# Softmax denominators by a transposing DMA and GpSimd in place of TensorE and VectorE, in an attention-then-MoE kernel on one Trainium2 core

## The chip, the cores and the metric

The kernel runs on one core of one Trainium2 chip. The metric is device time in microseconds, the median of the runs. Before the change it is 327.26 us, with runs from 327.18 to 327.89 us.

## The reference

For each of B = 4 batches there are N = 12544 rows of x with C = 128 channels, and m = 32 inducing vectors. An attention block is applied twice, and a small MoE layer follows.

```python
def mab(q, kv):
    s = scale * (q @ kv.transpose(0, 2, 1))
    s = s - s.max(-1, keepdims=True)
    a = np.exp(s)
    a /= a.sum(-1, keepdims=True) + 1e-09
    return a @ kv
h = mab(I, x)          # 32 rows per batch: I attends to x
y = mab(x, h)          # 12544 rows per batch: x attends to h
out = np.maximum(y @ w1, y @ w2) @ w_out      # d_ff = 1024
```

The denominators of the title are the sums over 32 entries in the second `mab`, one for each of the 50176 rows of x. They can be divided out at the very end, since all that follows is positively homogeneous.

## The kernel before

**Algebra.** max(h1, h2) is written as h1 + relu(h2 - h1). With H the 32 rows of h, the kernel makes `hwd` = H (w2 - w1), 32x1024, and `m1` = H w1 w_out, 32x128. For each chunk of 128 rows of x it needs E = exp(scores) (32x128), relu(hwd^T E) in eight pieces of 128 rows, the product of these with w_out, plus m1^T E, and at last a division by the denominators.

**Tiles.** A batch has 98 chunks. Up to 16 chunks make a block, four for each quarter of the 128 partitions: quarter q of tile `e2` (128x512, f16) has in its 32 partitions the exps of up to four chunks. There are 28 blocks, seven for each batch, numbered 0 to 27.

**Stages of a block.** `stage` (L577) multiplies the transposed x by H on TensorE (L591), and ScalarE makes `e2` by an exp (L603). `phase` (L932) issues four small products at a time, one in each quarter of TensorE's rows (L990). They give relu inputs in PSUM, which ScalarE (L1006) or VectorE (L1009) moves to SBUF, and also the product with `m1`. `final_one` (L797) issues the product with w_out, one matmul of 128 rows by 128 columns at a time (L809), up to 32 for a group of four chunks. `evict_group` (L826) multiplies the group by the reciprocal denominators `rp` on VectorE (L836) into an output tile `o`, and an output DMA on SyncE's queue (L861) sends it to HBM.

**The denominators.** `dens` (L626) is called by the first `final_one` of a block. For each chunk column it loads 128 columns of `e2` as weights and multiplies them by `ones_q` (128x4), so that four sums for 128 rows of x come out in PSUM (L641). It does two blocks at once where the next one is staged. VectorE takes the reciprocals (L651) into `rp`.

**The first attention** of batch b+1 runs beside the second attention of batch b. GpSimd's queue loads x by `load_x` (L160 to L165): seven DMAs per batch, which turn f32 into f16. They start after the copy L164, which waits for the last accumulation of the batch in hand (`pool_accum`, L348 to L403). SyncE's queue turns x by fourteen transposing DMAs per batch (L171), and the exps `eu` by six more (L345). Scores are made at L308, `pool_accum` at L364.

**What sets the order.** The program is recorded by hand. A planner keeps a clock of its own (`Clock`, L20), with a cost for each operation, and decides from it what TensorE does next: a phase, an output matmul, a block's staging or a piece of the first attention. A table `DEV` (L901) overrides single steps. Engines then take their instructions in the recorded order, and so do the queues: SyncE issues its DMAs one after the other, and a DMA that waits holds all that stand behind it. A tile pool with n buffers makes the first write of a buffer wait until the tile that had it n allocations ago is released. The output tiles have five buffers:

```python
outp = ctx.enter_context(tc.tile_pool(name="outp", bufs=5))
```

So the VectorE instruction that evicts a group waits until the output DMA of the group five before it has landed.

## Time and profile before

The profile is of one execution on the chip. The page gives its span, first to last instruction; its own time beyond the span isn't listed.

| what | before |
|---|---|
| median of three runs (lowest, highest) | 327.26 us (327.18, 327.89) |
| span of the profiled execution | 325.6 us |
| TensorE (PE) busy, share of the span | 319.8 us, 98% |
| VectorE (DVE) busy | 283.1 us, 87% |
| ScalarE (ACT) busy | 281.7 us, 87% |
| GpSimd (POOL) busy | 25.6 us, 8% |
| granted TensorE clock | 1.000 |
| DMA, mean over the span | 165 GB/s |

The page sums busy time by engine, follows back the chain of work that ended last, lists groups of instructions by line, and lists the DMA issues with the median time from issue to landing. PEld is TensorE's weight load, SPq SyncE's queue. A group's row reads: line, engine, operation, output and inputs with shapes, count, then busy time and mean ns of one, then idle time before it and what ended it. A row of the timeline begins with the start in us from the span's start and the duration in us.

### The profile page before, as it was taken

The numbers are of one execution on the slowest core, as the hardware profiler recorded it, in microseconds if no ns is written. First come the engines' busy times: TensorE is split into PE (matmuls) and PEld (weight loads), VectorE is DVE, ScalarE is ACT, GpSimd is POOL, SyncE is SP. The second block draws the span as 40 slices with busy tenths as digits, with TensorE's granted clock in tenths as the row PEclk, the third lists the DMA queues.
The fourth block names the chain that finished last, engine by engine and source line by source line (L and its number), as shares of the span: only waits on it lengthen the run. The fifth ranks groups of instructions, "written<-read, shape, count | busy, mean of one in ns | idle before, by whom it ended". The sixth has DMA issues, their size and how long they took to land.

```text
span 325.6 us, 12570 instructions
## 1 busy us (share of the span) xinstructions
PE 319.8 (98%) x5404; PEld 243.0 (75%) x5404; DVE 283.1 (87%) x509; ACT 281.7 (87%) x560; POOL 25.6 (8%) x51
## 2 busy tenths in 40 slices
PE   7999999999999999999999999999999999999996
PEld 3876777777767777777777777777777777778785
DVE  3359989989989998998989999998989999999973
ACT  3679899999989899998888999989969999999961
POOL 7452030000040000000040000000000000000000
PEclk9999999999999999999999999999999999999999
DMA  8999999976279999993389999992312312222233
GB/s 204 208 206 214 286 246 212 172 207 134 97 150 245 225 248 209 201 203 86 116 162 243 214 234 232 190 192 86 115 66 101 113 68 98 90 108 99 85 115 112
DMA packets 70823, 53.65 MB, mean 165 GB/s; under 512 B 52176, under 2 KB 55408, under 8 KB 70768
## 3 DMA queue, kind: packets, MB, share of 16 engines
q1 hardware_dynamic: 64656, 38.63, 49.2%
q0 software_dynamic: 6112, 14.22, 22.3%
q8 instruction: 42, 0.69, 0.9%
q14 instruction: 13, 0.11, 0.1%
HBM read 28.33 MB, written 25.69 MB: 166 GB/s over the span
## 4 chain that ended last, share of the span: by engine, by line
PE 95%; DVE 1%; DMA 1%; ACT 0%; issue 0%; ACTq 0%; DVEq 0%
PE ps L809 61%; PE ps L990 22%; PE ps L591 2%; PE ps L232 2%; PE ps L308 2%; PE ps L364 1%; DMA xf<-in_x_dram 1%; PE ps L248 1%; DVE relu L1009 1%; PE ps L280 1%; PE ps L641 1%; PE ps L766 1%; PE ps L271 1%; PE ps L657 0%; PE ps L473 0%; PE ps L409 0%
## 5 line engine op out<-in xcount | busy, mean ns | idle before, releaser
L1006 ACT ACTIVATE relu<-ps 128x512 f16<-128x512 f32 x461 | 244.8, 602 | 26.6 <-PE ps L990 18.1
L1009 DVE TENSOR_SCALAR relu<-ps 128x512 f16<-128x512 f32 x323 | 206.8, 682 | 16.9 <-PE ps L990 15.3
L809 PE MATMUL ps<-woutp,relu 128*128 128x128 f16 x3136 | 217.3, 220 | 0.0
L809 PEld LDWEIGHTS <-relu 128*128 128x128 f16 x3136 | 176.7, 98 | 39.6 <-issue 29.1
L990 PE MATMUL ps<-e,hwd 32*128 32x512 f16 (+2 forms) x880 | 88.7, 360 | 0.0
L836 DVE TENSOR_TENSOR o<-ps,rp 128x512 f32<-128x512 f32 (+3 forms) x108 | 68.5, 634 | 5.5 <-PE ps L809 3.4
L990 PEld LDWEIGHTS <-hwd 32*128 32x128 f16 x880 | 24.9, 91 | 21.1 <-issue 1.0
L990 PE MATMUL ps<-m,e 32*128 32x128 f16 x381 | 38.8, 217 | 0.0
L990 PEld LDWEIGHTS <-e 32*128 32x128 f16 x381 | 21.3, 93 | 2.6
L165 POOL DMA_DIRECT2D xn<-in_x_dram x31 | 17.0, 557 | 8.2 <-DMA xn<-in_x_dram 4.3
L236 DVE COPY xT<-ps 128x512 f16<-128x512 f16 (+3 forms) x11 | 5.5, 504 | 7.8 <-PE ps L232 7.7
L319 ACT ACTIVATE eu<-ps 128x512 f16<-128x512 f32 x18 | 10.8, 615 | 0.0
L603 ACT ACTIVATE e<-ps 128x512 f16<-128x512 f32 (+2 forms) x21 | 10.5, 577 | 0.0
L164 POOL COPY pace<-hacc 128x1 f32<-128x1 f32 x2 | 0.4, 184 | 114.8 <-DVE hacc L397 114.8
L591 PE MATMUL ps<-xT,hT 128*32 128x512 f16 (+3 forms) x114 | 8.9, 362 | 0.0
L239 ACT COPY xT<-ps 128x768 f16<-128x768 f16 (+3 forms) x11 | 6.1, 556 | 2.7 <-PE ps L232 2.6
L232 PE MATMUL ps<-identity,xn 128*128 128x128 f16 x98 | 7.4, 219 | 0.4 <-DVE xn L661 0.3
L232 PEld LDWEIGHTS <-xn 128*128 128x128 f16 x98 | 5.6, 97 | 1.6 <-DVE xn L661 1.1
L257 ACT ACTIVATE et<-ps 128x448 f16<-128x448 f32 (+4 forms) x11 | 4.5, 413 | 2.6 <-PE ps L248 2.6
L308 PE MATMUL ps<-xT,inducingT 128*32 128x512 f16 x72 | 6.5, 385 | 0.0
L591 PEld LDWEIGHTS <-hT 128*32 128x32 f16 x114 | 3.3, 94 | 4.1 <-issue 3.0
L364 PE MATMUL ps<-xn,eT 128*32 128x128 f16 x288 | 5.5, 220 | 0.0
(96 smaller groups left out, 108.2 us busy)
## 6 DMA issues: line engine op xcount, KB each, us to landing
out_dram<-o SPq DMA_DIRECT2D x90, 256.0 KB, 2.4
xn<-in_x_dram POOLq DMA_DIRECT2D x24, 448.0 KB, 11.8
out_dram<-o SPq DMA_DIRECT2D x10, 128.0 KB, 3.0
xn<-in_moe_w_dram POOLq DMA_DIRECT2D x4, 256.0 KB, 14.1
xn<-in_x_dram POOLq DMA_DIRECT2D x4, 224.0 KB, 10.2
xT<-xn SPq DMA_TRANSPOSE x42, 4.3
xf<-in_x_dram SPq DMA_DIRECT2D x1, 512.0 KB, 3.9
xf<-in_x_dram SPq DMA_DIRECT2D x1, 384.0 KB, 4.3
```

Of the source, the lines that this page charges most:

```text
L165: nc.gpsimd.dma_start(out=xn_at[b, i][:, 0:n, :], in_=xr[b, :, k0 : k0 + n, :])
L232: nc.tensor.transpose(ps[:, j, :], xn[:, g + j, :], identity16)
L308: nc.tensor.matmul(out=ps[32 * g : 32 * (g + 1), :], lhsT=inducingT, rhs=xT_tiles[b % 2][:, U * u + 4 * g : U * u + 4 * (g + 1), :], start ...
L319: nc.scalar.activation(out=eu, in_=ps, func=AF.Exp, scale=scale, accum_out=st[b]["es"][:, u : u + 1])
L364: nc.tensor.matmul(out=ps[32 * g : 32 * (g + 1), 0:128], lhsT=eT[:, j, 32 * g : 32 * (g + 1)], rhs=xn_of(b, U * v + 4 * g + j), start=(j = ...
L591: nc.tensor.matmul(out=ps[32 * q : 32 * (q + 1), 128 * t : 128 * (t + n)], lhsT=hq, rhs=xT[:, c : c + n, :], start=True, stop=True, tile_p ...
L603: nc.scalar.activation(out=blk.e2[:, 0 : 128 * wd], in_=ps[:, 0 : 128 * wd], func=AF.Exp, scale=st[0]["rs"] if blk.b == 0 else scale,)
L809: nc.tensor.matmul(out=g.ps[:, 128 * c : 128 * (c + 1)], lhsT=g.blk.relu[q][:, 128 * (jb * w4 + t) : 128 * (jb * w4 + t + 1)], rhs=woutp[: ...
L836: nc.vector.tensor_mul(osb[:, 0:n, :], g.ps[:, 0 : n * C].rearrange("p (s c) -> p s c", s=n), rp)
L990: nc.tensor.matmul(**seq[i])
L1006: nc.scalar.activation(out=dst, in_=src, func=AF.Relu)
L1009: nc.vector.tensor_scalar(out=dst, in0=src, scalar1=0.0, scalar2=None, op0=ALU.max)
```

## The change

From block 3 on, `dens` is not called. When a block has been staged, `turn_e2` issues a transposing DMA on SyncE's queue that turns `e2` into `ed` (two buffers): 128 rows of x on the partitions, and for each chunk column the four quarters' 32 exps along the row. GpSimd adds halves of 16, 8, 4, 2 and 1 entries (five instructions, through the tile `half`, which has one buffer), and a sixth raises the sums to the power -1 into `rd` (seven buffers), which takes the place of `rp` in `evict_group`. A block's turn is switched on by `turns_on`, a job that is due when 18 chunks are done, and which now also issues the subtraction `weights_1b` that stood before the main loop. Some constants (identity32, rep32, diag, the inducing vectors) move into a buffer that the relu tiles use later, which makes room in SBUF; `ones16` shrinks to two columns and `ones32`, which nothing read, goes.

```diff
+    edp = ctx.enter_context(tc.tile_pool(name="edp", bufs=2))
...
-    identity32 = consts.tile([128, 128], F32, name="identity32")
-    ones32 = consts.tile([128, 128], F32, name="ones32")
-    ones16 = consts.tile([128, 128], F16, name="ones16")
+    head = relup.tile([128, 4096], F16, name="head", tag="relu3").bitcast(F32)
+    identity32 = head[:, 0:128]
+    rep32 = head[:, 128:256]
+    ind_sb = head[0:M, 256:384]
+    diag = head[:, 384:416]
+    ones16 = consts.tile([128, 2], F16, name="ones16")
...
+    minus1 = consts.tile([128, 16], F32, name="minus1")
...
+        state = {"turn": False}
+
         def stage(blk):
...
             blk.staged = ck.bank[bi] = ck.on_act(end, 0.05 + wd * 128 / 1200.0)
+            if state["turn"]:
+                turn_e2(blk)
             blk.staged = max([blk.staged] + [st[qu.b].get("hwdr", 0.0) for qu in some])
+
+        def turn_e2(blk):
+
+            wd = blk.width
+            uid[0] += 1
+            ed = edp.tile([128, 4, 128], F16, name=f"ed_{uid[0]}", tag="ed")
+            nc.sync.dma_start_transpose(
+                ed[:, 0:wd, :], blk.e2[:, 0 : 128 * wd].rearrange("p (j t) -> p j t", j=wd)
+            )
+            den = edp.tile([128, 16], F32, name=f"den_{uid[0]}", tag="den")
+            half = edp.tile([128, 16, 16], F32, name=f"half_{uid[0]}", tag="half", bufs=1)
+            cur = ed[:, 0:wd, :].rearrange("p j (q m) -> p (j q) m", q=4)
+            n = M // 2
+            while n >= 1:
+                dst = half[:, 0 : 4 * wd, 0:n] if n > 1 else den[:, 0 : 4 * wd, None]
+                nc.gpsimd.tensor_tensor(out=dst, in0=cur[:, :, 0:n], in1=cur[:, :, n : 2 * n], op=ALU.add)
+                cur = half[:, 0 : 4 * wd, :]
+                n //= 2
+            rp = edp.tile([128, 4, 4], F32, name=f"rd_{uid[0]}", tag="rd", bufs=7)
+            nc.gpsimd.tensor_tensor(
+                out=rp[:, 0:wd, :].rearrange("p t q -> p (t q)"),
+                in0=den[:, 0 : 4 * wd],
+                in1=minus1[:, 0 : 4 * wd],
+                op=ALU.pow,
+            )
+            blk.rp = rp[:, 0:wd, :]
+            blk.turned = blk.staged
...
+        def turns_on():
+            weights_1b()
+            state["turn"] = True
...
         pending = []
+        at(18, turns_on)
...
+            if f is turns_on:
+                return True
...
         state["stage"] = 2
-        weights_1b()
         START = ck.pe
```

More of the change, by code (lines that the diff above doesn't have):

```diff
@@ L176 @@
     identity16 = consts.tile([128, 128], F16, name="identity16")
-    identity32 = consts.tile([128, 128], F32, name="identity32")
-    ones32 = consts.tile([128, 128], F32, name="ones32")
-    ones16 = consts.tile([128, 128], F16, name="ones16")
+    head = relup.tile([128, 4096], F16, name="head", tag="relu3").bitcast(F32)
[4 more added lines that the diff above has]
+    ones16 = consts.tile([128, 2], F16, name="ones16")
     warm = consts.tile([128, 512], F16, name="warm")
     ones_q = consts.tile([128, 4], F16, name="ones_q")
-    ind_sb = consts.tile([M, C], F32, name="ind_sb")
+    minus1 = consts.tile([128, 16], F32, name="minus1")
     w2h = relup.tile([128, 4096], F16, name="w2h", tag="relu0")[:, 0:J]
@@ L191 @@
     m1bd = consts.tile([128, 4, C], F16, name="m1bd")
-    rep32 = consts.tile([128, 128], F32, name="rep32")
     repd = consts.tile([128, 128], F32, name="repd")
-    diag = consts.tile([128, M], F32, name="diag")
     pace = consts.tile([128, 1], F32, name="pace")
@@ L214 @@
         nc.vector.memset(ones16, 1.0)
-        nc.vector.memset(ones32, 1.0)
+        nc.vector.memset(minus1, -1.0)
         nc.vector.memset(ones_q, 0.0)
@@ L724 @@
             g.blk.last_group[g.q] = n
-        state = {"g": 0, "mm": 0, "lin": 0, "done": 0, "issued": 0}
+        state.update({"g": 0, "mm": 0, "lin": 0, "done": 0, "issued": 0})
         ptr = [[0, 0] for _ in range(4)]
@@ L1046 @@
         pending = []
+        at(18, turns_on)
         def ready(f, a):
-            d = st[a[0]]
+            d = st[a[0]] if a else None
             now = ck.pe
+            if f is turns_on:
+                return True
             if f is pool_scores and a[1] >= NEU and ("eT", a[1] - NEU) not in d:
```

## The prediction

> **What bounds the kernel now.** I read the busy shares and the chain on the page first, then the groups by shape, the timeline where a denominator is made, and the DMA lists of single windows, since the change puts work on queues.

> ```profile
> PE 319.8 (98%) x5404; PEld 243.0 (75%) x5404; DVE 283.1 (87%) x509; ACT 281.7 (87%) x560; POOL 25.6 (8%) x51
> PE 95%; DVE 1%; DMA 1%; ACT 0%; issue 0%; ACTq 0%; DVEq 0%
> ```

> TensorE is the bound over the whole span: 95% of the chain is its own work, and it waits for almost nothing. So TensorE time taken away comes off the end, and a stall put in is added in full. VectorE and ScalarE have an eighth of their time free.

> **What goes.** These are the groups by shape, and the timeline of TensorE around eight denominator matmuls.

> ```profile
> L641 PE MATMUL ps<-ones_q,e 128*128 128x4 f16 x102 | 4.7, 165 | 0.0
> L651 DVE RECIPROCAL rp<-ps 128x32 f32<-128x32 f32 x9 | 3.1, 348 | 0.0
> L522 POOL TENSOR_TENSOR w<-xn,xn 128x512 f16<-128x512 f32 x2 | 2.5, 1270 | 10.3 <-DMA xn<-in_moe_w_dram 10.3
> ```

> ```profile
> 59.90 0.34 PE L641 MATMUL ps<-ones_q,e 128*128 128x4 f16 x8
> ...
> 60.11 0.27 PE L809 MATMUL ps<-woutp,relu 128*128 128x128 f16 x2
> ```

> The 165 ns of one matmul overlap. Eight of them delay the next output matmul from 59.90 to 60.11, so one costs 0.21 / 8 = 26 ns. The built program keeps 12 of the 102 (blocks 0 to 2), so 90 x 26 ns = **2.3 us** go. VectorE loses 13 of 15 reciprocals, some 13 x 0.32 = 4.2 us, and a PSUM bank is taken 13 times less. As nothing on TensorE waits for these, I count zero; at most they give 0.5 us.

> **What moves.** With dens gone the planner's clock runs differently. In the built order TensorE goes to column mode (staging, first attention) in three more visits; the rest of its counts stands. A change of mode leaves weight loads idle some 0.23 us (29.1 us over 124 waits "PEld L809 <- issue" in the list of waits). An extra visit costs one more change, and fewer returns elsewhere pay part: 0.4 us, between 0 and 0.7.

> **What is added.** There are 25 turns: 25 transposing DMAs on SyncE's queue and 150 GpSimd instructions. GpSimd's price has no row of its shape. The copy of one column took 184 ns (L164), the 512-column L522 1270 ns, so a line through both gives 2.1 ns per column: 0.73, 0.45, 0.32, 0.25, 0.22 us for the five adds and 0.22 for the power, 2.2 us in all. Bounds are six copies, 1.1 us, and six L522, 7.6 us. Over 325 us GpSimd has room. Nor is `rd` late by itself: the exps of blocks 7 to 10 begin at 93.9, and block 7's first eviction is at 108.2, the shortest such distance of a turned block.

> The cost is in **SyncE's queue**. `ed` has two buffers. Where three or four blocks are staged in a row, the third DMA must wait until the first has landed and GpSimd has read it, and the fourth for the second. All output DMAs behind them wait too, and with five `o` buffers the fifth eviction after the first held output stops VectorE, relus behind it included. So it counts how fast a turn lands. The first rows below are of the whole run; then come two lines of the issues between 90 and 113 us, while x for batch 2 is loaded; then DMA packets between 178.5 and 180.5 us, when a transpose runs beside the loads of batch 3.

> ```profile
> out_dram<-o SPq DMA_DIRECT2D x90, 256.0 KB, 2.4
> ...
> xT<-xn SPq DMA_TRANSPOSE x42, 4.3
> ...
> eT<-eu SPq DMA_TRANSPOSE x18, 2.8
> ```

> ```profile
> xn<-in_x_dram POOLq DMA_DIRECT2D x7, 448.0 KB, 13.1
> out_dram<-o SPq DMA_DIRECT2D x4, 256.0 KB, 8.0
> ```

> ```profile
> DMA packets 212, 0.43 MB, mean 214 GB/s; under 512 B 14, under 2 KB 103, under 8 KB 212
> ...
> q0 software_dynamic: 107, 0.37, 92.8%
> q1 hardware_dynamic: 105, 0.06, 13.9%
> ```

> A turn of 128x512 f16 is like eT: 2.8 us in quiet. Beside the loads the two queues get one packet each in turn, 105 against 107 in 2 us, 53 per us, whatever their size. Transposes move in 256-byte packets: 42 xT of 224 KB and 18 eT of 128 KB make 46848, and the page has 52176 packets under 512 B. A turn has 512, and needs 512 / 53 = **9.7 us** beside the loads.

> [...] The counts above speak for one against one.

> **Window A, 94 to 117 us.** In both programs blocks 7 to 10 are staged after the 664th output matmul, just behind the seven loads of batch 2 (issued 90.4 to 94.1, the last landing 19.6 us later, at 113.2). First turn: issued at 94.5, behind two outputs of 128 packets each, which are through between 96.8 (256 packets at 53 per us from 92) and 101.3 (issue of the second plus 8.0). I take 99; it lands at 108.7. GpSimd's first add ends at 109.4. The second turn gets the last of the loads' time and lands at about 112.2, the next add ends at 112.9, the fourth turn's issue (1.2 us, as eT's) at 114.1, and the first held output, issued in 0.3 us, lands 2.4 us later at 116.8. Which eviction waits for it:

> ```profile
> 95.03 0.42 DVE L836 TENSOR_TENSOR o<-ps,rp 128x256 f32<-128x256 f32 x1 [0.15 <-PE ps L809]
> ...
> 105.77 0.42 DVE L836 TENSOR_TENSOR o<-ps,rp 128x256 f32<-128x256 f32 x1
> ```

> The eviction of 95.03 is the first whose output stands behind the turns, and that of 105.77 is the fifth after it. VectorE is held from 105.8 to 116.8, 11.0 us. TensorE goes on for one round of a phase and output matmuls (1.1 us in the chain, phases at 105.99 and 107.14); the next phase needs the bank of the held eviction. Loss **9.9 us**, between 3 (turns landing twice as fast) and 13.

> **Window B, 165 to 183 us.** The new order makes batch 2's last accumulation after the 1356th output matmul (1381st before), so the loads of batch 3 start at about 161.3 and end by about 181. Blocks 14 to 16 are staged after the 1389th (1422nd before), exp at 165.1 instead of 167.9. First turn: 165.1 + 9.7 = 174.8, add 0.7, third turn issued at 176.8. Its outputs stand behind the second and third turn in the DMA queue, and the first lands at about 182.7. The fifth eviction, at 175.75 before, is held 6.9 us. Loss **5.8 us**, between 1 and 9.

> **Elsewhere** three turns in a row stand at blocks 21 to 23 and 24 to 26, with no loads about: the third waits 2.8 + 0.7 us, which five buffers bear. Between 47 and 66 us SyncE is full (outputs are issued up to 6 us behind their evictions), and the two turns put ahead of batch 1's tenth xT transpose delay it by 2 x 1.2 us. It landed at 59.5, and scores at 60.9 use it. For this and the like in batches 2 and 3 I add 1.5 us, between 0 and 4.

> **The sum**: -2.3 + 0.4 + 9.9 + 5.8 + 1.5 = +15.3 us on the profiled execution. Its span of 325.6 us lies 1.7 below the median of 327.26, and I add the change to the median: **342.6 us**. With all lower ends it is 328.5 (-2.8 + 0 + 3 + 1 + 0), with all upper ones 351.7 (-2.3 + 0.7 + 13 + 9 + 4).

> **Rivals.** First, the other side: the turns land in time and the gain stays. This is decided at window A: VectorE isn't held if 94.5 + L + 0.7 (add) + 1.5 (rest of that block's chain) + 0.7 + 1.2 + 0.3 + 2.4 is under 105.8, so if a turn lands in L < 4.5 us. For it speaks eT's 2.8 us (4.2 at most); against it that no eT was issued beside loads, and outputs there took 8.0. It gives 327.26 - 2.3 + 0.4 = 325.4 us. Second, only one window bites, since in B the queue starts empty and the third turn may go sooner: 327.26 - 2.3 + 0.4 + 9.9 + 1 = about 336. Third, GpSimd is slow: the power or the strided adds have no row. At the bound of 7.6 us per block the fourth turn goes out 5 us later and A costs 15: about 348. That the change doesn't do what it says is excluded by the built order: 12 denominator matmuls, 25 turns.

> **Chances.** Forecast 0.68 (333 to 351), one window 0.14 (328.5 to 337), slow GpSimd 0.05, hidden 0.13, in which small delays may eat the gain. From these: faster 0.10, same 0.03, slower 0.87, where 0.2% is about what a measurement of this kernel can tell from no change. The range 328.5 to 350 takes in the first two.

> **What would show it.** After: an eviction near 106 us that waits about 10 us for an output DMA, TensorE idle in that slice and near 176; a turn's landing median near 3 us but 10 us beside loads; output matmuls after L641 gone. Turns landing under 4.5 us beside loads would make it wrong.

## The result, and the profile after

The changed kernel takes 352.83 us (median of 5 runs, 352.26 to 353.45); the kernel before took 327.30 us beside it. The ratio is 1.077, with a 95% interval from 1.075 to 1.079. The change makes the kernel 25.5 us slower. The profiled execution took 352.83 us, with a span of 351.1 us.

The page, with the rows that answer to those shown of before, and with TensorE and its granted clock over the span in 40 slices of 8.8 us (a digit is tenths of busy time, or of full clock; 9 is 90% or more):

```profile
PE 323.8 (92%) x5314; PEld 243.9 (69%) x5314; DVE 281.2 (80%) x496; ACT 281.4 (80%) x560; POOL 137.1 (39%) x201
PE   8999999999992299999999199999999999999996
PEclk9999999999998589999999589999999999999999
PE 77%; DMA 13%; DVE 4%; POOL 2%; ACT 1%; issue 1%; SPq 1%; DVEq 0%; ACTq 0%
```

TensorE runs 90 matmuls less, yet is busy 4.0 us longer. Two holes stand out, in slices 13 and 14 and in slice 23, and in or just behind each the granted clock is lowered. In the chain, TensorE's share falls from 95% to 77% and DMA's rises from 1% to 13%. The list of waits names who waits in the holes (total, times, longest):

```profile
DVE o L869 <- DMA out_dram<-o: 21.9, 2, 13.5
PE ps L1023 <- DVE o L869: 20.5, 2, 12.7
```

VectorE waited twice for an output DMA to free an `o` buffer, and TensorE twice for VectorE to free the PSUM bank: 12.7 us and 7.7 us. Everything else is small: TensorE waited 0.7 us for an eT transpose and 0.6 us for an xT transpose. Here is the first hole on three engines: SyncE's queue, VectorE and TensorE.

```profile
95.27 22.70 SPq L621 DMA_TRANSPOSE ed<-e  x4
118.08 1.99 SPq L894 DMA_DIRECT2D out_dram<-o  x4
```

```profile
120.08 0.42 DVE L869 TENSOR_TENSOR o<-ps,rd 128x256 f32<-128x256 f32 x1 [13.51 <-DMA out_dram<-o]
```

```profile
107.44 0.23 PE L1023 MATMUL ps<-m,e 32*128 32x128 f16 x1
120.56 0.61 PE L1023 MATMUL ps<-e,hwd 32*128 32x512 f16 x2 [12.74 <-DVE o L869]
121.10 1.57 PE L842 MATMUL ps<-woutp,relu 128*128 128x128 f16 x13
```

Four turns hold the queue from 95.27 to 117.97. The outputs behind them go out from 118.08, the eviction that needs a buffer starts at 120.08, and TensorE goes on at 120.56. Thirteen output matmuls then take 1.57 us; 13 to 14 took 0.90 to 0.95 just before the hole. The table of windows shows why (length, then busy time and count of PE, PEld, DVE, ACT, POOL, then clock, DMA share, GB/s):

```profile
107.00:120.00 13.00, 0.82 (x11) 0.42 (x9) 0.00 (x0) 1.38 (x3) 8.31 (x12) 0.69 0.55 116
120.00:122.00 2.00, 1.44 (x14) 1.14 (x14) 1.92 (x4) 0.60 (x1) 1.93 (x2) 0.50 1.02 306
122.00:124.00 2.00, 2.00 (x20) 1.37 (x18) 1.72 (x4) 0.76 (x2) 1.67 (x5) 0.50 1.21 85
124.00:126.00 2.00, 2.00 (x25) 1.60 (x24) 1.24 (x2) 1.04 (x3) 2.00 (x1) 0.58 0.96 227
```

The mean of 0.69 over the 13 us of the hole means half clock for its last 8 us. From 120.56 to about 125.7 TensorE works at half its clock. Weighted by its busy time that costs 1.44 x 0.50 + 2 x 0.50 + 2 x 0.42 = 2.6 us; the same sum behind the second hole (200.2 to 204.1) gives 2.0. This takes it that the time is TensorE's in these stretches; the pauses put in below test that sum.

**The 25.5 us** are then: 20.5 waits for evictions, 4.6 lowered clock, 1.3 late transposes, and -1.1 for what the change removes (measured below). Together 25.3; the 4.6 and the 1.3 are worked out from this trace, and no run takes either away by itself.

### The profile page after: what moved, and what is told of

Same layout as the page of the kernel before. It is cut to its first block, busy times and chain, and to the rows that moved or that the text cites. A ratio compares the mean times of both kernels' runs of the same rounds, so it can differ in the third digit from the quotient of the medians.

```text
span 351.1 us, 12623 instructions
## 1 busy us (share of the span) xinstructions
PE 323.8 (92%) x5314; PEld 243.9 (69%) x5314; DVE 281.2 (80%) x496; ACT 281.4 (80%) x560; POOL 137.1 (39%) x201
## 4 chain that ended last, share of the span: by engine, by line
PE 77%; DMA 13%; DVE 4%; POOL 2%; ACT 1%; issue 1%; SPq 1%; DVEq 0%; ACTq 0%
PE ps L842 48%; PE ps L1023 18%; DMA ed<-e 8%; PE ps L234 2%; DVE relu L1042 2%; PE ps L595 2%; DMA eT<-eu 1%; POOL half L630 1%; DMA out_dram<-o 1%; PE ps L310 1%; DMA xf<-in_x_dram 1%; PE ps L366 1%; DVE o L869 1%; DMA xT<-xn 1%; POOL rd L634 1%
## 5 line engine op out<-in xcount | busy, mean ns | idle before, releaser
L842 PEld LDWEIGHTS <-relu 128*128 128x128 f16 x3136 | 179.2, 99 | 41.2 <-issue 30.8
L1023 PE MATMUL ps<-e,hwd 32*128 32x512 f16 (+2 forms) x880 | 91.0, 363 | 20.5 <-DVE o L869 20.5
L869 DVE TENSOR_TENSOR o<-ps,rd 128x512 f32<-128x512 f32 (+1 forms) x96 | 61.0, 638 | 28.2 <-DMA out_dram<-o 21.9
L634 POOL TENSOR_TENSOR rd<-den,minus 128x16 f32<-128x16 f32 (+2 forms) x25 | 66.6, 2662 | 2.0
L630 POOL TENSOR_TENSOR half<-ed 128x256 f32<-128x256 f16 (+2 forms) x25 | 15.4, 618 | 130.1 <-DMA ed<-e 130.1
L1023 PE MATMUL ps<-m,e 32*128 32x128 f16 x381 | 39.8, 219 | 0.0
L630 POOL TENSOR_TENSOR half<-half 128x32 f32<-128x32 f32 (+4 forms) x75 | 24.4, 326 | 5.9
L869 DVE TENSOR_TENSOR o<-ps,rp 128x512 f32<-128x512 f32 (+3 forms) x12 | 7.4, 614 | 0.0
L310 PE MATMUL ps<-xT,inducingT 128*32 128x512 f16 x72 | 6.7, 386 | 0.6 <-DMA xT<-xn 0.6
## 6 DMA issues: line engine op xcount, KB each, us to landing
out_dram<-o SPq DMA_DIRECT2D x90, 256.0 KB, 2.4
xn<-in_x_dram POOLq DMA_DIRECT2D x24, 448.0 KB, 11.5
xn<-in_moe_w_dram POOLq DMA_DIRECT2D x4, 256.0 KB, 13.8
```

Source lines behind the costliest of these rows:

```text
L630: nc.gpsimd.tensor_tensor(out=dst, in0=cur[:, :, 0:n], in1=cur[:, :, n : 2 * n], op=ALU.add)
L634: nc.gpsimd.tensor_tensor(out=rp[:, 0:wd, :].rearrange("p t q -> p (t q)"), in0=den[:, 0 : 4 * wd], in1=minus1[:, 0 : 4 * wd], op=ALU.pow,)
L842: nc.tensor.matmul(out=g.ps[:, 128 * c : 128 * (c + 1)], lhsT=g.blk.relu[q][:, 128 * (jb * w4 + t) : 128 * (jb * w4 + t + 1)], rhs=woutp[: ...
L869: nc.vector.tensor_mul(osb[:, 0:n, :], g.ps[:, 0 : n * C].rearrange("p (s c) -> p s c", s=n), rp)
L1023: nc.tensor.matmul(**seq[i])
```

## The experiments

All ratios are to the kernel before, run on the same chip.

### The removal alone, and GpSimd alone

In the first kernel the turns and the GpSimd work are left out.

```diff
-            ed = edp.tile(...)        # with the transposing DMA, the adds and the power
...
-            blk.rp = rp[:, 0:wd, :]
+            blk.rp = ones_rp[:, 0 : blk.width, :]
```

> The changed kernel without its 25 turns: no transposing DMA of e2 and no GpSimd sums; the division from block 3 on is by a constant tile of ones, so those blocks come out undivided. The TensorE order is that of the changed kernel. Theory (removal is worth 2.3 us, three more column visits cost 0.4, all of the loss comes from the turns): 325.4 us. Rival (part of the loss is in the new order, whose steps no longer fit the DEV table): 327.3 us or more.

Measured: 326.31 us, ratio 0.9965 (0.9952 to 0.9978), clock 1.000. What the change removes is worth 1.1 us, not 1.9: either the denominator matmuls cost less than 2.3 us or the new order more than 0.4, which this run does not part, nor from the constants and the subtraction that the change moved. All the rest of the loss comes with the turns.

The second kernel makes all 150 GpSimd instructions, on a constant tile, with no transposing DMA.

```diff
-            nc.sync.dma_start_transpose(ed[:, 0:wd, :], ...)
+            ed = ed_c
```

> The GpSimd sums and powers of the change, 150 instructions, on a constant tile of ones, without the transposing DMAs; the denominators from block 3 on are thus those of the constant and the division is wrong by that. Theory (GpSimd has room, and does not slow VectorE, whose work reads PSUM): as without turns, 326.3 us. Rival (GpSimd's 110 us of added work blocks VectorE or the loads that its queue issues): 328 us or more.

Measured: 326.12 us, ratio 0.9953 (0.9935 to 0.9971).

```profile
PE 318.6 (98%) x5314; PEld 240.9 (74%) x5314; DVE 280.9 (87%) x497; ACT 280.9 (87%) x560; POOL 136.7 (42%) x201
```

GpSimd is busy 136.7 us and costs nothing measurable: the time is that of the kernel without it.

### The DMAs alone, and the power

Here the 25 transposes stay and GpSimd's work goes; the outputs are divided by ones.

```diff
             nc.sync.dma_start_transpose(ed[:, 0:wd, :], ...)
-            den = edp.tile(...)       # with the adds and the power
...
-            blk.rp = rp[:, 0:wd, :]
+            blk.rp = ones_rp[:, 0 : blk.width, :]
```

> The 25 transposing DMAs with two ed buffers, but no GpSimd sums; the division from block 3 on is by ones, so those blocks come out undivided. Theory (the holds come from the landings beside the loads, GpSimd's chain of 4.9 us only lengthens the first): the fourth turn of window A goes at the landing of the second (113.3 us) and not at 116.8, the first held output lands near 117 instead of 119.8, window B wins the 0.7 us of one add; 352.8 - 3 - 0.8 = 349 us. Rival (GpSimd's slow chain is the main part): under 340 us.

Measured: 349.03 us, ratio 1.0640 (1.0608 to 1.0672). Its list of waits:

```profile
DVE o L855 <- DMA out_dram<-o: 18.1, 2, 10.1
PE ps L1009 <- DVE o L855: 16.6, 2, 9.3
```

Both holes stay, somewhat shorter. The transposes in SyncE's queue carry 21.6 of the 25.5 us by themselves. A third turn waits, for `ed`'s buffer, for the landing of the first, whether GpSimd reads it or not (25.3 us in 3 waits of the queue). GpSimd adds 3.8 us on top, and only where it stands between two turns. The next kernel splits that:

```diff
-                op=ALU.pow,
+                op=ALU.mult,
```

> GpSimd's power (2.66 us for each block) is replaced by a multiplication of the same shape, so the outputs are scaled by the sums instead of divided by them; all else is as in the changed kernel (352.8 us). The power stands between the first add of one turn and that of the next. Theory (a later turn waits for the adds and the power of the block before): GpSimd's step to the next turn's first add gets some 2.4 us shorter, so the fourth turn of the stage of 94 to 120 us goes out up to 2.4 us earlier, and TensorE's pause there falls from 12.7 to between 10.3 and 11.7 us; in the second stage, with three turns, only the first add is waited for, and nothing changes: 351.0 us, between 350.2 and 351.8. Rival (GpSimd isn't what the turns wait for; the landing of the transposes alone sets them): within 0.4 us of the changed kernel. The run with the transposes alone, at 349.0 us, bounds what all of GpSimd's work costs at 3.8 us.

Measured: 350.66 us, ratio 1.0729 (1.0686 to 1.0771). GpSimd's timeline in the changed kernel, then with the multiplication:

```profile
110.91 0.66 POOL L630 TENSOR_TENSOR half<-ed 128x256 f32<-128x256 f16 x1 [15.96 <-DMA ed<-e]
...
113.19 2.93 POOL L634 TENSOR_TENSOR rd<-den,minus 128x16 f32<-128x16 f32 x1
116.11 0.66 POOL L630 TENSOR_TENSOR half<-ed 128x256 f32<-128x256 f16 x1
```

```profile
112.35 0.66 POOL L630 TENSOR_TENSOR half<-ed 128x256 f32<-128x256 f16 x1 [16.56 <-DMA ed<-e]
...
114.63 0.22 POOL L634 TENSOR_TENSOR rd<-den,minus 128x16 f32<-128x16 f32 x1
114.80 0.67 POOL L630 TENSOR_TENSOR half<-ed 128x256 f32<-128x256 f16 x1
```

From one block's first add to the next it is 5.20 us with the power and 2.45 without. TensorE's first wait falls from 12.7 to 10.6 us, the second stays (7.7 before, 7.9 now by the total of 18.5). The power costs some 2 us, all of it in the one place where a fourth turn waits behind it.

### More buffers, and another queue

Four `ed` buffers instead of two; a small weight tile moves to make room.

```diff
-            ed = edp.tile([128, 4, 128], F16, ..., tag="ed")
+            ed = edp.tile([128, 4, 128], F16, ..., tag="ed", bufs=4)
```

> Four buffers for ed instead of two (w1T moves into the head tile to make room). Then no turn waits on SyncE for the landing of the one before the last. Theory 1 (the hold on SyncE by two buffers is the cause): both VectorE holds go, about 328 us. Theory 2 (behind it lies the DMA queue, in which 3 or 4 turns of 512 packets stand ahead of the outputs and get 53 packets per us beside the loads): the first output still lands only after the loads, near 115 instead of 120 us in window A and near 198 instead of 199.5 in window B; holds of 8 and 6.5 us stay, and with the slow clock after them about 346 us.

Measured: 346.36 us, ratio 1.0582 (1.0547 to 1.0617). Only 6.5 us come back, near the 346 us of the second theory. Its chain of waits in order of time (start, length, what), for 95 to 125 us:

```profile
98.64 8.81 SPq L622
...
107.56 3.20 SPq L622
...
110.85 4.38 DMA out_dram<-o
...
115.32 0.43 DVE o L870
```

No turn waits for a buffer any more, but the issue of the third turn itself takes 8.81 us, where its median over the run is 1.2, and that of the fourth 3.20. In this run the first two turns are issued in 1.5 and 1.3 us, and SyncE stands at the third until 107.46; the first lands at 111.6. The outputs go out at 110.85 instead of 118.08, which is still too late. So the buffer count was the smaller part of the hold, and the slow turns ahead in the same queue the larger: 15.0 us of TensorE's waits for evictions are left of 20.5.

In the next kernel, also with four buffers, the turns go out on ScalarE's queue.

```diff
-            nc.sync.dma_start_transpose(
+            nc.scalar.dma_start_transpose(
```

> The turns go out on ScalarE's queue instead of SyncE's, with four ed buffers as in the run with four buffers (346.4 us). Theory (the outputs are late because they stand behind the turns in SyncE's queue): an output no longer stands behind a turn, so both holds of VectorE go (waits of an output tile for its DMA under 1 us each), though the turns still land after 10 us or more beside the loads. ScalarE pays 25 issues of 1.0 to 1.3 us, some 30 us on top of 281, and four in a row take about 5 us, of which TensorE may wait for some 2 or 3 with its clock lowered afterwards: 332 us, between 327 and 342. Rival (the packets share the DMA engines, whatever the queue, so outputs are late anyway): the holds stay, at 6 us or more each, and the time is 345 us or more.

Measured: 412.78 us, ratio 1.261 (1.255 to 1.266), which both theories missed. The theory's mechanism held: the list of waits has no eviction waiting for an output DMA. Its price did not. Waits of SyncE's queue, and two rows of ScalarE:

```profile
SPq L172 <- DMA ed<-e: 18.8, 6, 4.4
```

```profile
52.37 1.32 ACTq L622 DMA_TRANSPOSE ed<-e  x1
53.74 3.04 ACT L1040 ACTIVATE relu<-ps 128x512 f16<-128x512 f32 x6 [8.16 <-issue]
```

An xT transpose on SyncE's queue now waits for a turn on ScalarE's, though neither touches the other's data, and eT does too (13.2 us in 4 waits). Turns seem to wait for xT in the same way: the turn at 52.37 goes out 3.4 us after the issue of an xT transpose at 48.96, and the next xT 2.6 us after the turn, at 54.97. ScalarE's relus stand behind a waiting turn, 8.2 us at this place. What makes transposes of two queues wait for each other the trace doesn't show. So this run tells that no eviction waits for an output when the turns go out on another queue, and that in this kernel a second queue for transposes was no way to get there.

### The clock

In the first kernel 100 and 60 dummy matmuls of 128 rows by 256 columns are put into the two holes, to keep TensorE at work.

```diff
+            for _ in range(state["hold"].pop(state["done"], 0)):
+                nc.tensor.matmul(out=groups[state["g"]].ps[:, 0:256], lhsT=warm[:, 0:128], ...)
```

> The changed kernel with 100 and 60 dummy matmuls of 128x256 (zeros added to the running group's PSUM bank) just ahead of the two phases at which TensorE stands still for 12.7 and 8.1 us. Theory (after standing still, TensorE is granted half of its clock for 4 to 5 us, which costs 2.5 + 2.0 us; 11 and 6.6 us of work in the stalls keep the clock): 352.8 - 4.5 = 348.3 us, with a granted clock of 1.00 in the slices after the holds. Rival (the clock falls for another reason, or the catching up of VectorE bounds these slices anyway): 352.8 us.

Measured: 352.28 us, ratio 1.0765 (1.0749 to 1.0781), only 0.5 us better. The dummies ended before the holes did, and what remained still lowered the clock, for 3.4 us behind each:

```profile
119.84 0.39 PE L1034 MATMUL ps<-e,hwd 32*128 32x512 f16 x2 [1.52 <-DVE o L870]
```

```profile
122.00:124.00 2.00, 2.00 (x22) 1.60 (x21) 2.00 (x4) 1.22 (x4) 1.77 (x4) 0.50 0.85 196
```

A pause of 1.5 us was followed by a clock of 0.50. Two stretches of 3.4 us at half clock cost 3.4 us, so this kernel could win 1.2 of the 4.6 us. It won 0.5, where its runs spread over 1.0 us; it doesn't decide between theory and rival. How short a pause lowers the clock, and what does that cost? The next two kernels have no turns (ones for the reciprocals) and make TensorE wait for a copy and memsets on GpSimd, first four times with long waits, then eight times with short ones.

```diff
+                nc.gpsimd.tensor_copy(out=slow[:, 0:128], in_=state["dst"])
+                for _ in range(n):                      # 1, 3, 5, 9; later one memset of 0 to 384 columns
+                    nc.gpsimd.memset(slow, 0.0)
+                nc.tensor.matmul(out=..., lhsT=slow[:, 0:128], rhs=warm[:, 0:128], ...)
```

> The kernel without turns (divided by ones from block 3 on) with four pauses of TensorE put in after the 2260th, 2340th, 2520th and 2620th output matmul, each by a matmul that waits for a GpSimd chain of a copy and 1, 3, 5 or 9 memsets of 0.54 us, behind the last relu. Theory (a pause of TensorE over some 1.5 us is followed by 3.4 to 6.8 us at half the granted clock): pauses of about 0.6, 1.7, 2.8 and 5 us, none after the first, half clock after the last two or three; span 323.9 + 10 + 2 to 3 us per lowered stretch = about 340 us. Rival (the clock falls only after holds of 10 us, or only where the DMA queues are full too): about 334 us, clock 1.00 throughout.

> As the kernel without turns (reciprocals replaced by ones from block 3 on) with four pauses, but with eight shorter ones: TensorE waits eight times for a copy on GpSimd and a memset of 0, 0, 128, 128, 256, 256, 384 and 384 columns. By the pause of 1.70 us behind a memset of 512 columns (0.52 us) and a copy (0.29 us), the idle times should be about 1.1 (twice), 1.3, 1.3, 1.45, 1.45, 1.6 and 1.6 us. If the clock goes down by a threshold in length between the 1.3 us that lowered nothing and the 1.70 us that did, the first ones show no lowered clock, the last ones 3.4 us each, and the span is 324 + 11 + 1.7 for each lowered stretch. If it goes by where the pause falls in a raster, some of a pair lower it and others of the same length don't.

Measured: 348.72 us with the long pauses, 337.41 with the short ones (one run each). The shortest of the long and the longest of the short, as the matmul behind each shows them:

```profile
248.24 0.23 PE L971 MATMUL ps<-warm,slow 128*128 128x128 f16 x1 [1.70 <-POOL slow L970]
```

```profile
299.18 0.23 PE L971 MATMUL ps<-warm,slow 128*128 128x128 f16 x1 [1.55 <-POOL slow L970]
```

After each of the four long pauses (1.70, 2.51, 3.85 and 6.31 us) the clock stood at half for 3.4, 3.4, 6.8 and 6.8 us. The pauses sum to 14.4 us and the span rose by 22.7 over the kernel without them, so some 8 us is the clock; half of TensorE's busy time in the lowered stretches, the sum used for the holes, gives 7.9. After the eight short ones (0.76 to 1.55 us, 9.5 in sum) it was never lowered, and the span rose by 11.5. So the rival of the long pauses (clock 1.00 throughout) fell, and the cost of the half clock was there with no turn and no load of x about. But length is no sharp bound: in the run on ScalarE's queue pauses of 1.36 and 1.41 us were followed by half clock for 3.4 and 6.8 us, and one of 1.56 us by none.

The traces tell more. The clock changes on a raster: in the changed kernel at 112.04, 125.70, 193.96 and 204.20 us, which are 4, 20 and 3 steps of 3.41 us apart. In the changed kernel and the one before, from where the clock is on record (6.23 and 4.75 us) to the step before that of the last matmul, the steps at full clock had matmuls for 2.60 us or more, but for the two that a lowering followed: 108.63 to 112.04 with 0.00 and 190.55 to 193.96 with 1.86. In other runs the steps ahead of a lowering had 1.71, 1.18, 1.09 and 0.00 us with the four long pauses, 1.86, 2.00 and 1.72 in three places of the run on ScalarE's queue (from 74.99, 252.49 and 344.65), and 1.89 at the first hole with the dummies. So in these runs it isn't the length of a pause alone that goes with a lowered clock, but how much of one step is idle. The pause of 1.41 us lay whole in the step from 252.49 to 255.90, busy for 2.00 of 3.41 us; that of 1.56 us was cut by an edge at 61.34, and the steps on both sides were busy for 2.56 and 2.70 us.

### Where turns do no harm

These kernels keep the denominators of some blocks on TensorE and VectorE. The first keeps the two stages with the holes (blocks 7 to 10 and 14 to 16).

```diff
+        KEEP = (7, 8, 9, 10, 14, 15, 16)
...
-            if state["turn"]:
+            if state["turn"] and blk.index not in KEEP:
```

> Blocks 7 to 10 and 14 to 16, which are staged beside the loads of x, keep their denominator matmuls; the other 18 of 25 are turned as in the change. Theory (the loss sits in these two windows alone): no holds, 62 of 90 matmuls saved, 327.3 - 62 x 0.026 + 0.4 + some 1.5 us of later xT and eT transposes = 327.6 us. Rival (turns cost on GpSimd or SyncE wherever they are): 335 us or more.

Measured: 334.96 us, ratio 1.0218 (1.0194 to 1.0241). The holes are gone, but 8 us remain, so the theory's 327.6 us fell. TensorE's timeline:

```profile
144.17 0.62 PE L366 MATMUL ps<-xn,eT 128*32 128x128 f16 x16 [2.86 <-DMA eT<-eu]
```

With the turns of other blocks in the queue, the first attention's eT transposes come late, a pause of 2.9 us follows, with half clock for some 6.7 us (by the mean of 0.990 over the span of 333.3). Whether these waits were covered by the holes before, or come from the order that this kernel has, is not told apart. The second keeps blocks 3, 4 and 7 to 16.

```diff
+        KEEP = (3, 4) + tuple(range(7, 17))
```

> Turned are only blocks 5, 6 and 17 to 27; blocks 3, 4 and 7 to 16 keep their denominator matmuls. So no turn stands beside loads of x, nor ahead of the xT and eT transposes of batches 1 and 2. 45 of 90 matmuls are saved. Theory (a turn costs only where SyncE's queue or the DMA queue is full): 327.4 - 45 x 0.026 + 0.8 (what the order cost without turns: 326.3 measured against 325.5) = 327.0 us, none of the holds, no wait of L310 or L366. Rival (turns in batch 3's stretch cost as well): 329 us or more.

Measured: 331.89 us, ratio 1.0128 (1.0111 to 1.0145). This missed the theory too: one single turn, of block 17, now stood beside the loads of batch 3 and landed after 13.6 us; VectorE waited 2.7 us for an output, TensorE 2.3 us for VectorE, and the granted clock was 0.993 over the span. The third keeps the blocks up to 20 and turns only 5, 6 and 21 to 27:

```diff
+        KEEP = (3, 4) + tuple(range(7, 21))
```

> Blocks 3, 4 and 7 to 20 keep their denominators on TensorE and VectorE; blocks 5, 6 and 21 to 27 are turned, which have no loads of x and few of the first attention's transposes beside them. Theory (a turn costs nothing where no load and no other transpose needs the queue): no hold, no pause of TensorE over 0.9 us, and the 33 denominator matmuls left out give 0.9 us less the changes of order: between 326.3 and 327.3 us. Rival (turns cost by themselves, for their packets or their issues): over 328 us, with a pause near 215 to 290 us.

Measured: 326.34 us, ratio 0.9967 (0.9954 to 0.9979).

```profile
PE 318.8 (98%) x5372; PEld 242.0 (75%) x5372; DVE 281.7 (87%) x504; ACT 281.4 (87%) x560; POOL 65.3 (20%) x105
```

Its nine turns land in 2.3 to 3.0 us, nothing waits for them, and it is as fast as the kernel that leaves the turns out. It beats both kernels, by 1.2 us over the one before, though it leaves out only 32 of the 90 matmuls. In this kernel, turns that have no load of x and few other transposes beside them do no harm.

## Why the prediction was wrong

The direction, the place and the mechanism were right: two holes, at the two predicted stages, from outputs behind turns beside the loads, through `o` buffers to VectorE and TensorE. The sum was +15.3 us and the result +25.5, above the top of the range. Three steps of the prediction failed. A pause of TensorE was charged by its length alone, with no term for the lowered clock behind it (4.6 us). A turn was taken to move as soon as it was issued, or at 99 in window A, while its first packet came 3.8 us after the issue in window B and at 100.4 in A. And GpSimd's power was taken for a copy (0.22 us; measured, 2.92). With the last two, TensorE's two waits came out 4.7 us longer than predicted. By the prediction's own steps:

- **What goes and what moves** (-2.3 + 0.4): measured together -1.1. That is 0.8 us less gain, from the matmuls or from the order.
- **GpSimd's price**, 2.2 us per block. The five adds were right to 0.1 us (0.67, 0.46, 0.32, 0.25, 0.22). The power was put at a copy's 0.22 us and takes 2.92 for 128x16; a line through a copy and a subtraction says nothing of a power. GpSimd as a whole stayed hidden as predicted, but in window A it set the fourth turn: its add began at 116.11, not at 112.2. The run without the power gives 2 us of this back.
- **A turn of 9.7 us beside the loads.** The rate was right, the start was not. These are the DMA packets from 101 to 105 us, then those from 181.25, when the first turn of window B was issued, to 183:

```profile
DMA packets 484, 0.83 MB, mean 207 GB/s; under 512 B 275, under 2 KB 275, under 8 KB 482
...
q0 software_dynamic: 237, 0.74, 92.5%
q1 hardware_dynamic: 245, 0.06, 12.3%
```

```profile
DMA packets 118, 0.37 MB, mean 209 GB/s; under 512 B 16, under 2 KB 16, under 8 KB 118
...
q0 software_dynamic: 118, 0.37, 110.2%
```

  The first shows one packet for one, as predicted (q0 carries the loads, q1 what SyncE issues). The view that the prediction read this from held no transpose's packets, though: 89 of its packets lie between 512 B and 2 KB, and a transpose's have some 250 (0.06 MB in 245 above), so they were those of an output. In the second nothing of SyncE's queue moves, and so it stays until 185. From there to 194.4 us it moves 542 packets beside 551 of the loads, and the first turn lands at 195.4: 14.2 us instead of 9.7, of which 3.8 are the wait for the first packet. What delays it the trace doesn't show. In window A the turn stands behind outputs, and its first packet comes at 100.4 and not 99; from there to 109.8 it is 559 beside 558, and the turn lands at 110.8. Once the loads were over, 846 packets of this queue went in 2.5 us, so the second turn landed at 113.3.
- **Window A**, 9.9 us: measured 12.7. The hold began 0.8 us later than predicted and ended 3.3 us later. The fourth turn waited for the second add, which began at 116.11 and not at 112.2: 1.1 us of that is the landing of the second turn (113.3 for 112.2), 2.8 are GpSimd's chain. The output then landed some 0.5 us sooner after its issue than allowed for.
- **Window B**, 5.8 us: measured 7.7. Here the first landing was 4.5 us later against its issue, and from it to the output's landing 4.3 us passed where I had added 7.9.
- **Elsewhere**, 1.5 us: measured 1.3. Right in the sum, but perhaps by luck: with the two stages kept, the other turns cost 8 us.
- **The clock** was left out. The 4.6 us behind the two holes had no term. With the two windows' 2.8 + 1.9 us, the 0.8 us of the first step above, and 0.2 less elsewhere, this is the 10 us between forecast and result.

Of the rivals, the hidden turns fell (a turn needed to land within 4.5 us and took 15.6), and so did the single window. "Slow GpSimd" came nearest in time, and its mechanism, a fourth turn that goes out later, was there in part: GpSimd's work between turns cost 3.8 us, the power 2 of them. The run of GpSimd alone shows that it costs nothing without the turns.

## What to carry to other kernels

When a change adds a DMA to a queue that also carries outputs, ask what that queue's last landing will be beside the heaviest load, for all pieces in flight together, and how far the output buffers reach; more buffers for the new DMA moved the wait to its issue here (8.81 us for the third turn). Price a pause of TensorE with its clock: here the two holes and the four long pauses put in, 1.70 to 12.7 us, were each followed by 3.4 us or more at half speed, and so were pauses of 1.36, 1.41 and 1.52 us, where 41% or more of one 3.41 us step was idle. And put such a DMA only where its queue is quiet: nine turns of 25 gave the same time as leaving all of them out.
